# A chunked gated-linear-attention and adapter-mixture kernel: order of all engines from a list scheduler in the kernel, and the recurrent state kept in PSUM

## The chip, the cores and the metric

The kernel runs on one core of one Trainium2 chip. The metric is device time in microseconds (us) of one execution. The engines of the core are TensorE (PE: matmuls; PEld is its weight load), VectorE (DVE), ScalarE (ACT), GpSimd (POOL) and SyncE (SP, which here only issues DMA transfers). Each engine works through its own instructions strictly in the order in which the kernel emitted them, and waits where an input or a buffer is not ready. A *unit* below is one batch and one chunk of 128 time steps.

## The reference

Inputs are q, k, v and alpha, each of 4 batches x 8 heads x 768 steps x 48 elements, and the weights of a small mixture of adapters. Cut to what matters:

```python
for t in range(S):                                   # S = 768, per batch and head
    state = alpha[:, :, t, :, None] * state + k_t (x) v_t      # 48 x 48
    y[:, :, t] = q_t @ state
x = y as (3072, 384)                                 # 8 heads x 48
logits = x @ w_gate                                  # 8 experts, the best 2 kept
w = softmax of the two best logits
out = x + sum over chosen experts e of w_e * (x @ A[e]) @ B[e]   # rank 16
```

## The kernel before

There are 24 units: 4 batches of 6 chunks. Within a unit, `ln` takes log(alpha) on ACT, and `cum` sums the logs of later steps with one matmul against a triangular matrix `suf` (columns 0 to 383 of a PSUM tile) and the sum over the whole chunk with four matmuls against a column of ones. ACT makes `up` = exp(cum), `dn` = exp(-cum) and `dec` = exp(total). POOL makes `kg` = k*up (`kgm`), `qg` = q*dn (`qgm`) and a bf16 copy of v (`vbc`). PE transposes kg and qg, two heads at a time (`tr`, 8 transposes), DVE copies them out (`kq`), PE forms the 128 x 128 products of keys and queries of each head (`at`, 8 matmuls), DVE multiplies them by the causal mask into `at_sb` (`msk`).

The output of a unit, `y`, is a PSUM tile that collects three things: the query against the decayed state (`qs`, L292), the masked products against v (`av`, L303) and at the end the adapters' part (`delta`, L382). Between the second and the third lies a serial chain through three engines: `xb` (ACT) - `xt` (PE) - `xs` (ACT) - `z` (PE) - `zc` (ACT) - `mx`, `df` (DVE) - `ex` (ACT) - `wu`, `rd`, `zw` (DVE) - `zt` (PE) - `zs` (ACT) - `delta` (PE) - `fin` (ACT, the copy `o<-y`, L389) and the store (SP, L391). There are two buffers for y, one for `at`, five for o, and four shared ones in PSUM (tag "m") for cum, tr, kv, xt, z and zt.

The state: `kv` (L249) multiplies kg by v for two heads at once, so each of its four 128 x 96 results holds two wanted 48 x 48 blocks and two that mix heads. `state` (L262, L264) reads the wanted blocks with two DVE instructions (64 partitions x 192), adds `sdec` and writes them into the bf16 tile `sbd`, whose cross-head blocks were zeroed once. `sdm` (L221) makes `sdec` = sbd*dec on POOL. All of this occurs only where a chunk follows in the batch.

What sets the order: one list, `STEP`, of 32 pairs of a stage and an offset. Step n emits each stage for unit n + offset, so for instance step n holds `av` of unit n, `z` to `fin` of unit n-1, `tr` to `msk` of unit n+1 and the POOL products of units n+2 and n+3. Loads: batch 0 comes by chunk (24 transfers of 196.6 KB), batches 1 to 3 by tensor (alpha, k, q, v; 1.18 MB each). Eight chunk loads are issued from ACT after its table load, five weight loads and then all other loads of batch 0 and batch 1 from SP; from step 0 on each step appends one store and one more load to SP.

## Time and profile before

| | |
|---|---|
| three runs | 143.31, 142.85, 141.25 us; median 142.85 |
| the profiled execution | 143.36 us, of which the span from first to last instruction is 141.6 |
| busy in the span | PE 86.2 us, DVE 96.5, ACT 77.0, POOL 77.8 |
| DMA | 24.18 MB; read 19.28, written 4.72 |
| y copied out (`o<-y`), start | unit 0 at 33.11, unit 3 at 48.44, unit 20 at 126.58, unit 23 at 138.33 us |

The busy times are unions over the whole span, so they average a head that loads bound, a long middle and a tail. The start times of `o<-y` mark how far the units have come: 17 units pass between 48.44 and 126.58 us, 4.60 us each. In the views below, a line of the chain of waits has start, length and what the end of the program waited for; a group's line has instructions, busy time and mean nanoseconds of one, and the idle time in front with what ended it.

### The profile page before, as it was taken

How to read it: one execution, taken by the hardware profiler on the slowest of the kernel's cores; microseconds unless marked ns; L12 is line 12 of the kernel's file. 1: busy time of each engine (PE TensorE's matmuls, PEld its weight loads, DVE VectorE, ACT ScalarE, POOL GpSimd, SP SyncE). 2: the span in 40 equal slices, each digit the busy share in tenths (PEclk: the TensorE clock that was granted, in tenths of full speed). 3: DMA queues.
4: the chain of work that ended last, by engine and by line, in shares of the span. 5: the costliest groups of instructions: out<-in, count | busy, mean ns of one | idle time of the engine just before them, and what ended most of it. 6: DMA issues, size and time to landing. Idle time of an engine off the chain costs nothing.

```text
span 141.6 us, 2947 instructions
## 1 busy us (share of the span) xinstructions
PE 86.2 (61%) x1048; PEld 63.9 (45%) x1048; DVE 96.5 (68%) x236; ACT 77.0 (54%) x232; POOL 77.8 (55%) x111
## 2 busy tenths in 40 slices
PE   0002049919664997998868846577597649596330
PEld 0001037708443855866746624455374437473210
DVE  1110016946995687889889798789897998989530
ACT  3002545346582674776765857567467647555431
POOL 8000299618564775676785757748767478521200
PEclk9999999999995555555797799968959995959955
DMA  4999999968998829695985969892110111001111
GB/s 74 231 255 259 235 210 201 285 181 231 282 249 229 248 78 272 173 267 152 299 224 173 276 190 309 239 366 68 62 58 9 46 60 56 36 20 60 56 56 56
DMA packets 50718, 24.18 MB, mean 171 GB/s; under 512 B 29072, under 2 KB 50704, under 8 KB 50704
## 3 DMA queue, kind: packets, MB, share of 16 engines
q1 hardware_dynamic: 42384, 22.43, 58.1%
q10 hardware_dynamic: 8320, 1.57, 5.5%
q8 instruction: 8, 0.13, 0.4%
q14 instruction: 6, 0.05, 0.1%
HBM read 19.28 MB, written 4.72 MB: 169 GB/s over the span
## 4 chain that ended last, share of the span: by engine, by line
DVE 30%; DMA 19%; ACT 18%; SPq 16%; PE 9%; issue 5%; POOL 1%; ACTq 0%; POOLq 0%
SPq L88 8%; DVE kq L240 8%; SPq L91 8%; DVE zw L366 8%; DMA v_t<-in_v_dram 7%; DVE df L343 6%; ACT o L389 5%; DMA out_dram<-o 5%; ACT up L184 4%; DMA q_t<-in_q_dram 4%; PE zt L373 4%; DVE wu L354 3%; DMA W_st<-in_moe_A_dram 3%; ACT zc L333 3%; ACT zs L378 3%
## 5 line engine op out<-in xcount | busy, mean ns | idle before, releaser
L208 POOL TENSOR_TENSOR qg<-q_t,dn 128x384 bf16<-128x384 f32 x24 | 24.0, 999 | 23.8 <-ACT dn L189 23.8
L281 DVE TENSOR_TENSOR at_sb<-at,mask 128x1024 bf16<-128x1024 f32 x24 | 29.2, 1216 | 3.6 <-PE at L273 3.6
L240 DVE COPY kq<-tr 128x1024 bf16<-128x1024 bf16 x24 | 16.6, 690 | 13.1 <-PE tr L234 12.5
L221 POOL TENSOR_TENSOR sdec<-sbd,dec 128x384 bf16<-128x384 bf16 x20 | 16.6, 828 | 15.1 <-DVE sbd L264 12.9
L201 POOL TENSOR_TENSOR kg<-k_t,up 128x384 bf16<-128x384 f32 x24 | 24.0, 1001 | 0.9 <-ACT up L184 0.9
L215 POOL CAST vb<-v_t 128x384 bf16<-128x384 f32 x24 | 12.1, 503 | 14.0 <-PE kv L249 9.7
L173 PE MATMUL cum<-lg,suf 128*128 128x384 bf16 x24 | 10.9, 456 | 12.6 <-ACT lg L163 12.6
L234 PE MATMUL tr<-ident,kg 128*128 128x128 bf16 x96 | 12.9, 277 | 5.8 <-POOL kg L201 5.8
L378 ACT COPY zs<-zt 128x128 bf16<-128x128 bf16 x24 | 6.4, 266 | 16.5 <-PE zt L373 16.5
L273 PE MATMUL at<-kq 48*128 48x128 bf16 x192 | 12.1, 261 | 4.9 <-DVE kq L240 4.6
L348 ACT ACTIVATE ex<-df 128x8 f32<-128x8 f32 x24 | 5.0, 208 | 18.4 <-DVE df L343 18.4
L373 PE MATMUL zt<-ident,zw 128*128 128x128 bf16 x24 | 6.1, 254 | 14.4 <-DVE zw L366 14.4
L366 DVE SCALAR_TENSOR_TENSOR zw<-zc,rd,wu 128x128 bf16<-128x128 f32 x24 | 13.9, 580 | 0.8
L175 PEld LDWEIGHTS <-lg 128*128 128x128 bf16 x96 | 7.5, 116 | 14.0 <-issue 13.5
L292 PE MATMUL y<-sdec,kq 128*128 128x96 bf16 x80 | 8.3, 240 | 8.7 <-POOL sdec L221 8.0
L189 ACT ACTIVATE dn<-cum 128x384 f32<-128x384 f32 x24 | 11.5, 478 | 3.7 <-PE cum L175 3.5
L310 ACT CAST xb<-y 128x384 bf16<-128x384 f32 x24 | 11.4, 473 | 3.9 <-PE y L303 3.6
L264 DVE TENSOR_TENSOR sbd<-kv,sdec 64x192 bf16<-64x192 f32 x32 | 11.2, 351 | 3.1 <-PE kv L249 2.9
L234 PE MATMUL tr<-ident,qg 128*128 128x128 bf16 x96 | 12.7, 274 | 0.0
L389 ACT COPY o<-y 128x384 f32<-128x384 f32 x24 | 11.8, 494 | 1.6 <-PE y L382 1.0
L343 DVE TENSOR_SCALAR df<-zc,mx 128x8 f32<-128x8 f32 x24 | 11.7, 486 | 0.8
L184 ACT ACTIVATE up<-cum 128x384 f32<-128x384 f32 x24 | 12.2, 506 | 0.0
(45 smaller groups left out, 180.9 us busy)
## 6 DMA issues: line engine op xcount, KB each, us to landing
out_dram<-o SPq DMA_DIRECT2D x24, 192.0 KB, 2.5
v_t<-in_v_dram SPq DMA_DIRECT2D x5, 192.0 KB, 4.0
k_t<-in_k_dram SPq DMA_DIRECT2D x4, 192.0 KB, 3.7
q_t<-in_q_dram SPq DMA_DIRECT2D x4, 192.0 KB, 4.6
a_t<-in_alpha_dram ACTq DMA_DIRECT2D x3, 192.0 KB, 3.7
a_t<-in_alpha_dram SPq DMA_DIRECT2D x3, 192.0 KB, 3.8
k_t<-in_k_dram ACTq DMA_DIRECT2D x2, 192.0 KB, 4.9
q_t<-in_q_dram ACTq DMA_DIRECT2D x2, 192.0 KB, 4.3
```

Source lines behind the costliest of these rows:

```text
L184: nc.scalar.activation(s["up"].rearrange("p h d -> p (h d)"), s["cum"][:, 0:DM], AF.Exp)
L201: nc.gpsimd.tensor_tensor(out=s["kg"][:, :, 0:D], in0=batches[b][1][:, c], in1=s["up"], op=ALU.mult)
L208: nc.gpsimd.tensor_tensor(out=s["qg"][:, :, 0:D], in0=batches[b][2][:, c], in1=s["dn"], op=ALU.mult)
L215: nc.gpsimd.tensor_copy(out=s["vb"], in_=batches[b][3][:, c])
L221: nc.gpsimd.tensor_tensor(out=sdec[c % 2].rearrange("p a b d -> p a (b d)"), in0=sbd[c % 2].rearrange("p a b d -> p a (b d)"), in1=_bc(s[" ...
L234: nc.tensor.transpose(t[:, w, p, :], pair(src, p), ident[:, :])
L240: nc.vector.tensor_copy(out=s["kq"], in_=s["tr"])
L273: nc.tensor.matmul(t[:, hh, p, :], s["kq"][rows, 0, p, :], s["kq"][rows, 1, p, :], start=True, stop=True)
L281: nc.vector.tensor_tensor(out=s["at_sb"].rearrange("p a b t -> p (a b) t"), in0=s["at"].rearrange("p a b t -> p (a b) t"), in1=_bc_mid(mas ...
L343: nc.vector.tensor_scalar(s["df"], s["zc"][:, E * R:NW], s["mx"][:, 0:1], None, ALU.subtract)
L366: nc.vector.scalar_tensor_tensor(out=s["zw"], in0=s["zc"][:, 0:E * R].rearrange("p (e r) -> p e r", e=E), scalar=s["rd"][:, 0:1], in1=_bc( ...
L389: nc.scalar.copy(o, s["y"])
```

## The change

1. **Order.** `STEP` goes. A function `graph` lists each stage of each unit as a node with an engine, an occupancy and a latency in ns (`STAGES`), with data dependences (`CHAINS`) and buffer reuse (`RINGS`, `HOLDS`). `list_order` then simulates the engines: it repeatedly picks, on the engine that can start first, among the nodes that can start within 40 ns of the first one, the one with the lowest unit number less `LEAD` of its stage. The four shared PSUM buffers are handed out in that order. `plan` sorts everything by planned start, the loads by 7 us less than theirs, and the kernel emits in that order; stores become nodes of their own.
2. **State.** `state`, `sbd` and POOL's `sdm` go. `kv` now begins (for chunks 1 to 4) with one matmul of the identity against `sdec`, 128 x 384, and adds the four products onto it, so the PSUM tile holds the whole new state, cross-head blocks included. The next unit's `sdm` is one DVE product of that PSUM tile (128 x 384, f32) with a `dec` of 8 columns, into bf16 `sdec`. In the 8 columns, a small matmul of `sel` and `gap` puts -1000 where rows and head do not match, so exp gives 0 there.
3. **cum** also gets one matmul of 512 columns of zeros (`warm`) at its start, overwritten by what follows.
4. kg and qg have 4 buffers in place of 3; the first loads of k and v go on ACT, before the table load, all others on SP; the casts of the adapters' weights move behind `msk` of unit 1 on DVE.

In the order that results, y is worked on by pairs: in most of the list, ACT, for instance, has xb, xs, zc, ex, zs and o of one unit each beside the same stage of the next. On DVE a `kq`, `msk` or `sdm` stands between the pair's small instructions. Behind the six units of batch 0, DVE has kq, kq, msk, kq, msk of units 6 to 8 before the first instruction that needs v of batch 1. On SP, the store of unit 0 stands ahead of the loads of k and q of chunk 5, that of unit 1 ahead of v of chunk 5 and alpha, k and q of batch 1, those of units 2 and 3 ahead of v of batch 1; the stores of units 6 and 7 stand behind alpha of batch 3, and from unit 10 on only stores are left.

The diff, cut:

```diff
-RING = 3
+RING = 4
...
+STAGES = {
+    "ln": ("ACT", 445, 545), "ln2": ("ACT", 765, 865),
+    "cum": ("PE", 513, 680), "edn": ("ACT", 385, 485), "eup": ("ACT", 360, 485),
+    "edec": ("ACT", 98, 172), "kgm": ("POOL", 979, 1024), "qgm": ("POOL", 979, 1024),
+    "vbc": ("POOL", 419, 464), "tr": ("PE", 450, 620), "kq": ("DVE", 595, 679),
+    "sdm": ("DVE", 497, 581), "kv": ("PE", 340, 500), "at": ("PE", 400, 570),
+    "msk": ("DVE", 1164, 1248), "qs": ("PE", 170, 340), "av": ("PE", 215, 385),
+    "xb": ("ACT", 385, 485), "xt": ("PE", 170, 340), "xs": ("ACT", 360, 485),
+    "z": ("PE", 180, 350), "zc": ("ACT", 153, 278), "gmx": ("DVE", 91, 175),
+    "gdf": ("DVE", 76, 160), "gex": ("ACT", 107, 232), "gwu": ("DVE", 268, 352),
+    "grd": ("DVE", 71, 155), "gzw": ("DVE", 258, 342), "zt": ("PE", 57, 220),
+    "zs": ("ACT", 147, 272), "delta": ("PE", 163, 330), "fin": ("ACT", 385, 485),
+    "st": ("DMA", 655, 2455),
+}
+LEAD = {
+    "vbc": 4.27, "ln": 3.98, "cum": 4.66, "edn": 3.24, "eup": 2.43, "edec": 2.5, "kgm": 2.57,
+    "qgm": 3.55, "tr": 2.34, "kq": 0.1, "sdm": 0.93, "kv": 1.48, "at": -2.91, "msk": -0.66,
+    "qs": 0.66, "av": 0.85, "xb": 0.02, "xt": 0, "xs": 1.6, "z": 0.29, "zc": 1.6, "gmx": -0.26,
+    "gdf": 0.17, "gex": -0.25, "gwu": -0.88, "grd": -1.01, "gzw": 0.71, "zt": 2.42, "zs": 0.57,
+    "delta": -0.7, "fin": -3.99, "st": 100,
+}
+CHAINS = (
+    "ln cum eup kgm tr kq at msk av xb xt xs z zc gmx gdf gex gwu grd gzw zt zs delta fin st",
+    "cum edn qgm tr", "cum edec sdm kv", "kgm kv", "vbc kv", "sdm qs av", "kq qs", "vbc av",
+)
+RINGS = (
+    ("kgm", "eup", 2), ("qgm", "edn", 2), ("sdm", "edec", 6), ("tr", "kgm", RING), ("kv", "kgm", RING),
+    ("tr", "qgm", RING), ("kv", "vbc", 3), ("av", "vbc", 3), ("at", "kq", 3), ("qs", "kq", 3),
+    ("msk", "at", 1), ("av", "msk", 2), ("fin", "qs", 2), ("fin", "av", 2), ("xt", "xb", 3),
+    ("z", "xs", 3), ("delta", "zs", 3), ("st", "fin", 5), ("qs", "sdm", 2), ("kv", "sdm", 1),
+    ("kgm", "cum", 2), ("qgm", "cum", 2), ("at", "tr", 3), ("qs", "tr", 3), ("z", "xt", 3),
+    ("gzw", "z", 3), ("delta", "zt", 3), ("edec", "kv", -1), ("qs", "kv", 1),
+)
+HOLDS = {
+    "cum": (("eup", 0), ("edn", 0), ("edec", 0)), "tr": (("kq", 0),), "kv": (("sdm", 1),),
+    "xt": (("xs", 0),), "z": (("zc", 0),), "zt": (("zs", 0),),
+}
+SLOTS = 4
+READER = ("ln", "kgm", "qgm", "vbc")
+HANDOVER = {"PE": 53, "DVE": 35, "ACT": 35, "POOL": 35, "DMA": 600, "DMB": 600}
...
+def list_order(nodes, deps, holds):
...
+    slot, place, rel = [0] * SLOTS, {}, {}
...
+        best = None
+        for e, names in cand.items():
+            can = []
+            for n in names:
+                if n[0] == "ld" and loads[e][nl[e]][1] != n:
+                    continue
+                s = max(ready[n], free[e])
+                if n in holds:
+                    if slot[ns % SLOTS] is None:
+                        continue
+                    s = max(s, slot[ns % SLOTS])
+                can.append((s, n))
+            if can:
+                first = min(can)[0]
+                if best is None or first < best[0]:
+                    s, n = min((x for x in can if x[0] <= first + 40),
+                               key=lambda x: (nodes[x[1]][3], x[0]))
+                    if best is None or s < best[0]:
+                        best = (s, n, e)
+        if best is None:
+            return 1e9, order
+        s, n, e = best
+        cand[e].remove(n)
+        nl[e] += n[0] == "ld"
+        if n in holds:
+            place[n], slot[ns % SLOTS] = ns % SLOTS, None
+            ns += 1
...
+        for a in owner.get(n, ()):
+            left[a] -= 1
+            k = place[a]
+            rel[a] = max(rel.get(a, 0), end + 53)
+            if left[a] == 0:
+                slot[k] = rel[a]
+        for b in succ[n]:
+            eb = nodes[b][0]
+            if eb == e:
+                w = free[e] if e in ("PE", "DMA", "DMB") else end
+            else:
+                w = end + HANDOVER[eb]
+            ready[b] = max(ready[b], w)
+            wait[b] -= 1
+            if wait[b] == 0:
+                cand[eb].append(b)
...
+    return out[:8] + ["w"] + out[8:]
+
+
+def load_engine(x):
+    return "ACT" if x in ((0, 1, 0), (0, 3, 0)) else "SP"
...
+        for line in CHAINS:
+            names = line.split()
+            for f, g in zip(names, names[1:]):
+                dep((f, u if has(f, u) or f != "ln" else u - 1), (g, u))
+        for f, g, d in RINGS:
+            dep((f, u - d), (g, u))
+        dep(("kv", u - 1), ("sdm", u))
...
+        t = 1060 if c is not None else 4500
+        nodes[n] = ("DMB" if eng == "POOL" else "DMA", t, t + 1300, x)
...
+def plan(lead=LEAD):
+    nodes, deps, holds = graph(lead)
+    span, order = list_order(nodes, deps, holds)
+    start = {n: s for s, n in order}
+    before = {}
+    for a, b in deps:
+        before.setdefault(b, []).append(start[a])
+    keyed = []
+    for k, (s, n) in enumerate(order):
+        if n[0] == "ld":
+            if ("is", n[1]) in nodes:
+                continue
+            s = max([s - 7000] + before.get(n, []))
+        elif n[0] == "is":
+            n = ("ld", n[1])
+        keyed.append((s, k, n))
+    return span, [n for _, _, n in sorted(keyed)]
...
+    order = plan()[1]
+    early = [n for n in order if n[0] == "ld"][:8]
+    for n in early:
+        ld(n[1])
+    nc.scalar.preload_act_table_set("natural_log_exp_and_others")
...
+    def wcast(_):
+        nc.vector.tensor_copy(out=W, in_=W_st)
+        nc.vector.tensor_copy(out=B_all, in_=B_st)
...
+    sel = consts.tile([P, 2, HP], F2, name="sel")
+    nc.vector.memset(sel, 0.0)
+    gap = consts.tile([P, NP, 2], F2, name="gap")
+    nc.vector.memset(gap, 0.0)
+    for i in range(2):
+        nc.vector.memset(sel[HP * i:HP * i + 1, i, :], 1.0)
+        nc.vector.memset(gap[HP * i:HP * i + 1, :, 1 - i], -1000.0)
...
+    sdec = [consts.tile([P, NP, 2, D], F2, name=f"sdec{i}") for i in range(2)]
...
+        for _ in range(1):
+            nc.tensor.matmul(cum, suf[:, :], warm[:, :], start=True, stop=True)
         nc.tensor.matmul(cum[:, 0:DM], suf[:, :], lg[:, :, 0:D], start=True, stop=True)
+        nc.tensor.matmul(
+            cum[:, DM:DM + H], sel.rearrange("p a b -> p (a b)"),
+            gap.rearrange("p a b -> p (a b)"), start=True, stop=False,
+            skip_group_check=True)
         for p in range(NP):
             nc.tensor.matmul(
-                cum[:, DM + p:DM + p + 1],
+                cum[:, DM + 2 * p:DM + 2 * p + 2],
                 lg[:, 2 * p:2 * p + 2, :].rearrange("a b s -> a (b s)"), ones[:, :],
-                start=True, stop=True)
+                start=False, stop=(p == NP - 1), skip_group_check=True)
...
+        s["dec"] = scal.tile([P, H], F4, name="dec", bufs=6)
+        nc.scalar.activation(s["dec"], s["cum"][:, DM:DM + H], AF.Exp)
...
     def sdm(u):
-        s = st[u]
         b, c = units[u]
         if c > 0:
-            nc.gpsimd.tensor_tensor(
-                out=sdec[c % 2].rearrange("p a b d -> p a (b d)"),
-                in0=sbd[c % 2].rearrange("p a b d -> p a (b d)"),
-                in1=_bc(s["dec"][:, :], 2 * D), op=ALU.mult)
+            nc.vector.tensor_tensor(
+                out=sdec[c % 2].rearrange("p a b d -> p (a b) d"),
+                in0=st[u - 1].pop("kv").rearrange("p a b d -> p (a b) d"),
+                in1=_bc(st[u]["dec"][:, :], D), op=ALU.mult)
...
+        if c > 0:
+            nc.tensor.matmul(
+                s["kv"].rearrange("p a b d -> p (a b d)"), ident[:, :],
+                sdec[c % 2].rearrange("p a b d -> p (a b d)"),
+                start=True, stop=False, skip_group_check=True)
         for p in range(NP):
             nc.tensor.matmul(
                 s["kv"][:, p].rearrange("p b d -> p (b d)"), pair(s["kg"], p), pair(s["vb"], p),
-                start=True, stop=True)
-
-    def state(u):
-        s = st[u]
-        b, c = units[u]
-        if c + 1 == NCH:
-            return
-        for hh in range(2):
-            rows = slice(HP * hh, HP * hh + HP)
-            dst, src = sbd[(c + 1) % 2][rows, :, hh, :], s["kv"][rows, :, hh, :]
-            if c == 0:
-                nc.vector.tensor_copy(out=dst, in_=src)
-            else:
-                nc.vector.tensor_tensor(
-                    out=dst, in0=src, in1=sdec[c % 2][rows, :, hh, :], op=ALU.add)
...
+        if c == 0:
+            s["y"] = ps_y.tile([P, DM], F4, name="y")
...
-        o = outp.tile([P, DM], F4, name="o")
-        nc.scalar.copy(o, s["y"])
+        s["o"] = outp.tile([P, DM], F4, name="o")
+        nc.scalar.copy(s["o"], s["y"])
+
+    def store(u):
-        nc.sync.dma_start(out=out[t0:t0 + C, :], in_=o)
+        nc.sync.dma_start(out=out[t0:t0 + C, :], in_=st[u]["o"])
...
-    STEP = (
...
-    with tc.manual_schedule():
-        for n in range(-6, NU + 3):
-            for f, off in STEP:
-                u = n + off
-                if 0 <= u < NU:
-                    f(u)
-            for _ in range(1 if n >= 0 else 0):
-                if queue:
-                    load(*queue.pop(0))
+    for n in order:
+        if n not in early:
+            emit[n[0]](n[1])
```

## The prediction

> **What bounds the kernel now.** I read the slices of the span first, then the chain of waits in order of time, then the windows of a middle stretch, then the groups, and last single instructions in the timeline.
>
> The slices (3.54 us each) show two regimes:
>
> ```profile
> DVE  1110016946995687889889798789897998989530
> ...
> PEclk9999999999995555555797799968959995959955
> DMA  4999999968998829695985969892110111001111
> ```
>
> Up to about 44 us the DMA row is full while no engine is; from slice 14 on DVE is at 8 or 9 and the DMA row falls off. The chain names the hinge between the two, and one later stall:
>
> ```profile
> 34.23 10.04 DMA v_t<-in_v_dram
> 44.39 0.37 POOL vb L215
> 44.85 0.87 POOL sdec L221
> ...
> 82.85 7.03 DMA out_dram<-o
> 89.96 0.48 ACT o L389
> ```
>
> The first line: everything waits for v of batch 1, landed at 44.3 us. POOL, in order, holds `sdec` of unit 4 behind `vb` of unit 6, so the units of batch 0 wait for a load that they don't need: `o<-y` of unit 3 starts only at 48.44. The fourth line: a store queued behind loads holds an o buffer.
>
> Two stretches of the middle (us, busy time and count of PE, PEld, DVE, ACT, POOL, then clock, DMA share, GB/s):
>
> ```profile
> 50.00:82.00 32.00, 26.52 (x311) 19.98 (x310) 27.43 (x68) 22.23 (x69) 22.23 (x27) 0.65 0.74 216
> 91.60:126.00 34.40, 24.29 (x318) 18.04 (x319) 30.79 (x74) 21.31 (x69) 22.02 (x27) 0.82 0.25 85
> ```
>
> At 4.60 us a unit (front table), DVE's 86% and 90% are 3.94 and 4.12, mean 4.03 us a unit: it is the fullest engine, but it idles 0.57. The rest of the pace is in-order waiting; the chain there hops DVE - PE - ACT through the mixture. The groups that the change touches:
>
> ```profile
> L281 DVE TENSOR_TENSOR at_sb<-at,mask 128x1024 bf16<-128x1024 f32 x24 | 29.2, 1216 | 3.6 <-PE at L273 3.6
> ...
> L221 POOL TENSOR_TENSOR sdec<-sbd,dec 128x384 bf16<-128x384 bf16 x20 | 16.6, 828 | 15.1 <-DVE sbd L264 12.9
> ...
> L366 DVE SCALAR_TENSOR_TENSOR zw<-zc,rd,wu 128x128 bf16<-128x128 f32 x24 | 13.9, 580 | 0.8
> ...
> L264 DVE TENSOR_TENSOR sbd<-kv,sdec 64x192 bf16<-64x192 f32 x32 | 11.2, 351 | 3.1 <-PE kv L249 2.9
> ...
> L343 DVE TENSOR_SCALAR df<-zc,mx 128x8 f32<-128x8 f32 x24 | 11.7, 486 | 0.8
> ```
>
> L343 works on 8 columns and takes 486 ns in the mean; its shortest is 231 and its longest 754. L366 has 350 and 1105. The short ones lie beside an idle POOL, the long ones beside POOL products; L281 stays within 1210 to 1225 either way.
>
> **The change, part by part.** I sum up to the landing of v of batch 1, then 18 units at a pace, then the end.
>
> *Head, 47.6 us.* The bytes ahead of v of batch 1 decide. Before: 24 chunk loads (4.72 MB), batch 1 (4.72) and weights (0.4), 9.84 MB by 44.3 us; the window 13 to 44 us shows 240 GB/s, so this stretch is transfer alone. The change keeps these bytes and puts four stores (4 x 196.6 KB = 0.79 MB, 3.3 us at 240 GB/s) ahead of that v: 44.3 + 3.3 = 47.6. Bounds: 44.3 if stores cost the loads nothing; above, SP waits in order for the copies of y. It reached k of chunk 5 at 19.6 us; in the new order unit 0's copy I put at about 22 (first log at 4.5 instead of 12.0 us, since ACT no longer issues eight loads first; then the rows of its chain, 17 us with both casts and `msk` of unit 1 in front of `z`). Queued behind it are all later loads. 2.4 us there and as much at unit 1 give 52.4 if no backlog covers it; each transfer waits only for the one eight places ahead of it, so a backlog is likely, and I take 47.6.
>
> In exchange, the six units of batch 0 need no v of batch 1 any more. They begin some 8 us earlier, and 6 x 4.6 = 28 us from about 9 us plus one chain end near 40, inside the load wait. Before, only units 0 to 2 were out by then. The earlier start itself gains nothing beyond this: the load hides it.
>
> *State.* Removed: two DVE instructions in 20 units, 0.71 us together in the timeline (351 each), and POOL's 828 ns. Added on DVE: one product of 384 PSUM elements, not in the trace. Below: 0.351 (L264, 192 elements, also PSUM); above: 0.71, the two removed. Between L264 and L281 an element costs (1216 - 351)/(1024 - 192) = 1.04 ns, so 351 + 192 x 1.04 = 551 ns; I take that. Over 24 units: 20/24 x (0.551 - 0.71) = -0.13 us a unit (bounds -0.30 and 0). POOL loses 0.69 a unit, 16.6 in all; it was at 69% and isn't the bound, but its products stretch DVE: mean over shortest is 0.255 (L343), 0.07 (L354) and 0.23 (L366), 0.56 a unit. POOL's products fall from 2.69 to 2.0 us a unit, so by that share 0.14 goes (bounds 0 and 0.56). DVE: 4.03 - 0.13 - 0.14 = 3.76 us a unit.
>
> *PE.* By the shapes a unit streams 4764 columns; added are 512 (`warm`), 12 (`gap` and wider ones) and 16/24 x 384 (identity), 5544 in all. The timeline prices a column:
>
> ```profile
> 99.15 0.39 PE L234 MATMUL tr<-ident,kg 128*128 128x128 bf16 x4
> ...
> 104.04 0.63 PE L234 MATMUL tr<-ident,kg 128*128 128x128 bf16 x4
> ```
>
> One last matmul is 219 and 314 ns, so the starts lie 57 and 105 ns apart: 0.44 ns a column at full clock, 0.83 at half. 5544 columns are 2.4 or 4.6 us. At full clock this lies beside DVE; at half it is a bound of its own. Before, the clock stood at half from 41.9 to 69.2 us with PE busy for over 80% (the fives above), and then mostly full. With 16% more columns PE is nearly without a pause when cold, so I take full clock for most of the middle; the bounds are 0 and +0.87 us a unit (4.63 - 3.76).
>
> Here a rule is weighed: the Trainium skill, "TensorE: Matmul & The Clock Gate", Part 1, says that one window of about 3.4 us of sustained matmuls releases the throttle. This trace agrees only in part, since 27.3 us at over 80% did not release it. By the rule the sum below stands as it is; by the row taken to the end it becomes the cold rival.
>
> *Order.* Which limit is next? The y chain of a pair: two buffers, each held from `qs` to `fin`. By the groups and the timeline at full clock: 0.33 + 0.36 + 0.47 + 0.33 + 0.48 + 0.35 + 0.30 + 0.17 + 0.49 + 0.21 + 0.36 + 0.16 + 0.58 + 0.23 + 0.27 + 0.34 + 0.49 = 5.9 us. The last unit shows the handovers: from `zc` at 135.14 to the end of `o` at 138.81 is 3.67, its rows are 3.25, so 0.04 each; 16 make 0.6. The partner ahead on ACT costs about 0.47, and one DVE product in between (0.69 to 1.22) about 1.0. A pair takes 5.9 + 0.6 + 0.5 + 1.0 = 8.0, 4.0 a unit, above DVE's 3.76. Pace 4.0; bounds 3.76 (DVE without a gap) and 4.60 (the order gains nothing).
>
> The store stall at 82.85 goes: when SP meets the stores of units 6 and 7, four loads are queued ahead, and o has five buffers. It is inside the 4.60. `ident` and `warm` at cum cost DVE and ACT nothing at full clock; RING 4 and the moved casts are in the head.
>
> *Sum.* 47.6 + 0.6 (`vb`, 503 ns, and a handover) + 9 x 8.0 + 2.8 (end of the last `o` at 138.81 to the span's end) = 123.0; outside the span lie 143.36 - 141.6 = 1.76: 124.8 on the profiled execution's footing. The median is 0.4% below that execution, so **124.3 us**, forecast 124. Units 6 to 8 enter with some DVE work done; the last pairs have no DVE work beside them; I set neither off.
>
> **Rivals.**
> 1. *The order gains nothing* (18%): the planner's times are too short for the chip (`gzw` 258 against 580, `gdf` 76 against 486), so engines wait in order as now. 47.6 + 0.6 + 18 x 4.60 + 2.8 + 1.76 = 135.6. For: L343 and L366 vary by POOL; against: the waits of DVE are mostly for ACT within one unit's chain (10.5 us before `mx`), which pairing fills.
> 2. *DVE alone bounds, the stores are free* (14%): 44.3 + 0.6 + 18 x 3.76 + 2.8 + 1.76 = 117.1.
> 3. *PE stays at half clock* (8%): 4.63 us of columns a unit; between 53.08 and 67.14 us, all cold, three units passed at 4.69 against 4764 x 0.83 = 3.98 of columns, 1.18 times. 4.63 x 1.18 = 5.46, and 47.6 + 0.6 + 98.3 + 2.8 + 1.76 = 151: slower than before. It decides from a pace of (142.85 - 52.8)/18 = 5.0. For: that stretch; against: later windows are mostly full.
> 4. *The plan doesn't do what it says*: loads wait on stores at SP and the head grows to 52.4 or more. At pace 4.0 that is 129.6, inside my main case.
>
> **How the numbers follow.** Main case 118 to 131: 60%. The range reaches from rival 2 to rival 1 with its bounds: 115 to 136, leaving out rival 3, the slower half of rival 1 and a little below. A difference under 2% (140.0 to 145.7) can't be told from no change. Rival 3 gives slower 6% and part of same; same 4%; faster 90%.
>
> **What would show it.** Right: v of batch 1 landing at 45 to 50 us with units 0 to 5 copied out before; `o<-y` in pairs about 8 us apart; DVE near 94% in the middle; no L221 on POOL; the product of PSUM near 0.55 us; `df` shorter; full clock. Wrong: transposes 107 ns apart all through the middle (rival 3), `o<-y` 9 us apart a pair (rival 1), DMA idle before 45 us while SP waits for `o` (rival 4).

## The result and the profile after

| | before | after |
|---|---|---|
| median, us | 142.77 (4 runs, 141.25 to 143.31) | 167.25 (4 runs, 166.16 to 167.69) |
| span of the profiled execution, us | 141.6 | 164.4 |
| busy in the span: PE, DVE, ACT, POOL, us | 86.2, 96.5, 77.0, 77.8 | 98.2, 86.8, 79.5, 61.3 |
| v of batch 1, end of its last packet, us | 43.9 | 63.8 |
| last load, end of its last packet, us | 93.4 | 126.4 |

The ratio is 1.172, 95% interval 1.162 to 1.183: slower by 17%, where 124 us was forecast. The last two rows count the packets of the loads in order of time; the completion that an engine waits for comes at 44.3 and 65.4 us for v of batch 1, and at 93.8 and 127.2 for the last load. Executions more than 1.5% above the fastest of the same kernel are left out of all ratios here; the profiled ones of e3, g2, g4 and h1 below are such, so a difference of that size in their rows says nothing.

No engine got fuller: the busiest, PE, has 60% of the span. The slices of the kernel after (4.11 us each; the GB/s row is what the DMA engines moved):

```profile
DVE  1025756767120046656870389487547795768050
PEclk9999999879655558597895699598765985859555
DMA  6998999999999999969997999999999402020202
GB/s 104 163 146 145 175 141 181 213 201 164 170 157 169 206 184 168 165 167 184 167 165 151 162 164 188 191 169 182 180 187 234 153 0 100 0 96 0 96 0 96
```

The DMA row is at 9 in nearly all of the first 31 slices, some 127 us; before, the DMA engines were busy in the first 27, about 96 us, and not full in all of them. DVE never stays at 9. And the full DMA engines move only some 170 GB/s (169 in the median of those slices). The two stretches that were shown of before, in the same columns:

```profile
50.00:82.00 32.00, 19.35 (x233) 13.88 (x231) 15.41 (x30) 13.59 (x38) 13.93 (x17) 0.70 1.00 176
91.60:126.00 34.40, 23.66 (x304) 17.05 (x306) 23.17 (x53) 21.09 (x64) 16.93 (x21) 0.80 1.05 178
```

In the first, the DMA engines had a share of 0.74 at 216 GB/s before, now 1.00 at 176; DVE fell from 27.43 to 15.41 us of 32. The queue of the loads and stores (packets, MB, share of 16 engines' span), first before and then after:

```profile
q1 hardware_dynamic: 42384, 22.43, 58.1%
```

```profile
q1 hardware_dynamic: 48624, 23.61, 83.4%
```

The bytes are the same (q10 lost what q1 gained, since some first loads moved from ACT to SP), but 58.1% of 141.6 us is 82 us and 83.4% of 164.4 is 137. The chain of waits in order of time (start, length, what) has three long links:

```profile
41.01 16.03 DMA q_t<-in_q_dram
...
72.68 16.40 DMA q_t<-in_q_dram
...
109.64 9.88 DMA q_t<-in_q_dram
```

One for each of the batches 1 to 3. The groups say who waits, and that the operations themselves cost what they should:

```profile
L429 POOL TENSOR_TENSOR kg<-k_t,up 128x384 bf16<-128x384 f32 x24 | 24.0, 1000 | 37.1 <-DMA k_t<-in_k_dram 26.7 <-ACT up L410 10.3
L436 POOL TENSOR_TENSOR qg<-q_t,dn 128x384 bf16<-128x384 f32 x24 | 23.7, 998 | 16.6 <-DMA q_t<-in_q_dram 16.5
...
L448 DVE TENSOR_TENSOR sdec<-kv,dec 128x384 bf16<-128x384 f32 x20 | 11.0, 549 | 3.1 <-PE kv L481 3.1
...
L585 DVE SCALAR_TENSOR_TENSOR zw<-zc,rd,wu 128x128 bf16<-128x128 f32 x24 | 9.7, 404 | 0.6
...
L562 DVE TENSOR_SCALAR df<-zc,mx 128x8 f32<-128x8 f32 x24 | 9.0, 375 | 0.4
```

So the loads became slow at the same bytes. The trace records each packet, a piece of a transfer that one DMA engine moves at a time. The 768-byte ones (four runs of 192 bytes, loads of batches 1 to 3) took 42 ns in the median before and 79 after. The 192-byte ones (one run each, loads of batch 0) took 15 and 16 in the median, but 15.2 and 22.7 in the mean: before they are nearly all at 15, after they spread from 13 to 46. The 1536-byte ones of the stores took about 66 in the median of both. What changed is what writes into SBUF in 192-byte runs.

That points at the load tiles. They hold 192 of every 256 bytes (`load`, `[P, H * NCH, 64]` in f32). In the built programs they start in each partition at byte 35648 before and 37472 after, 64 and 96 beyond a multiple of 256. A run from 64 ends at 256; a run from 96 crosses it and ends at 288. The tiles ahead moved them by 1824 bytes: `warm` +1024, `sel` +256, two more `kg`/`qg` +2048, `sbd` gone -1536, and `gap`, 16 bytes that take 32. Only the last isn't a multiple of 256.

### The profile page after: what moved, and what is told of

The parts are those of the page before. It is cut to its first block, busy times and chain, and to the rows that moved or that the text cites. A ratio compares the mean times of both kernels' runs of the same rounds, so it can differ in the third digit from the quotient of the medians.

```text
span 164.4 us, 3023 instructions
## 1 busy us (share of the span) xinstructions
PE 98.2 (60%) x1106; PEld 67.5 (41%) x1112; DVE 86.8 (53%) x221; ACT 79.5 (48%) x228; POOL 61.3 (37%) x93
## 3 DMA queue, kind: packets, MB, share of 16 engines
q1 hardware_dynamic: 48624, 23.61, 83.4%
## 4 chain that ended last, share of the span: by engine, by line
DMA 30%; PE 23%; DVE 11%; ACT 11%; POOL 9%; SPq 7%; issue 7%; ACTq 0%; DVEq 0%; POOLq 0%
DMA q_t<-in_q_dram 26%; SPq L302 6%; POOL qg L436 5%; DMA a_t<-in_alpha_dram 4%; PE tr L461 4%; POOL kg L429 4%; PE y L601 3%; DVE wu L573 2%; PE y L522 2%; PE xt L535 2%; DVE at_sb L499 2%; DVE zw L585 2%; ACT xb L529 2%; PE cum L395 2%; PE y L509 2%
## 5 line engine op out<-in xcount | busy, mean ns | idle before, releaser
L461 PE MATMUL tr<-ident,qg 128*128 128x128 bf16 x96 | 12.8, 276 | 15.2 <-POOL qg L436 15.2
L540 ACT COPY xs<-xt 128x384 bf16<-128x384 bf16 x24 | 11.6, 482 | 10.4 <-PE xt L535 10.3
L461 PEld LDWEIGHTS <-qg 128*128 128x128 bf16 x96 | 8.9, 127 | 16.3 <-POOL qg L436 16.3
L557 DVE MAX8 mx<-zc 128x8 f32<-128x8 f32 x24 | 4.0, 166 | 18.2 <-ACT zc L552 18.0
L601 PE MATMUL y<-B_all,zs 128*128 128x384 bf16 x24 | 11.0, 458 | 3.8 <-ACT zs L597 3.8
L461 PE MATMUL tr<-ident,kg 128*128 128x128 bf16 x96 | 12.3, 267 | 1.6 <-POOL kg L429 1.3
L522 PE MATMUL y<-vb,at_sb 128*128 128x48 bf16 x192 | 10.6, 201 | 3.8 <-DVE at_sb L499 2.5
L546 PE MATMUL z<-W,xs 128*128 128x136 bf16 x72 | 10.1, 262 | 4.4 <-ACT xs L540 3.3
L535 PE MATMUL xt<-ident,xb 128*128 128x128 bf16 x72 | 10.2, 265 | 4.2 <-ACT xb L529 4.0
L448 DVE TENSOR_TENSOR sdec<-kv,dec 128x384 bf16<-128x384 f32 x20 | 11.0, 549 | 3.1 <-PE kv L481 3.1
L573 DVE SCALAR_TENSOR_TENSOR wu<-zc,mx,ex 128x8 f32<-128x8 f32 x24 | 9.3, 388 | 5.4 <-ACT ex L567 5.3
```

Source lines behind the costliest of these rows:

```text
L461: nc.tensor.transpose(t[:, w, p, :], pair(src, p), ident[:, :])
L522: nc.tensor.matmul(s["y"][:, h * D:(h + 1) * D], s["at_sb"][:, hh, p, :], s["vb"][:, h, :], start=(c == 0 and h == 0), stop=False, skip_gr ...
L535: nc.tensor.transpose(s["xt"][:, i, :], s["xb"][:, i * P:(i + 1) * P], ident[:, :])
L573: nc.vector.scalar_tensor_tensor(out=s["wu"], in0=s["zc"][:, E * R:NW], scalar=s["mx"][:, 1:2], in1=s["ex"], op0=ALU.is_ge, op1=ALU.mult, ...
L601: nc.tensor.matmul(s["y"], s["zs"][:, :], B_all[:, :], start=False, stop=True, skip_group_check=True)
```

## Experiments 1 to 4: where the load tiles lie

A tile that nobody reads moves the load tiles, and with them every tile that is allocated behind it, by as many bytes. Apart from the one memset of that tile, no instruction and no order changes. With 112 elements it is 224 bytes:

```diff
+    shift = consts.tile([P, 112], F2, name="shift")
+    nc.vector.memset(shift, 0.0)
     suf = consts.tile([P, P], F2, name="suf")
```

The others differ in the size: 16 elements (32 bytes) and 96 (192) in the kernel after, 16 in the kernel before.

> The changed kernel, with an unused tile of 224 bytes per partition ahead of its other constants, so that the load tiles start at 64 modulo 256 bytes in their SBUF partition, where they stood before the change; in the changed kernel they start at 96. Nothing else differs, and no computation is left out. Theory 'place': the start of the 192-byte runs that the loads write sets the DMA rate. Then 768-byte packets take 42 ns again in the median (79 in the changed kernel), loads move at about 240 GB/s, v of batch 1 lands near 48 us and the time falls from 167 to between 118 and 136 us. Rival 'queue': it is the new issue order (nearly all loads on SP, stores in between) that slows the packets. Then they still take near 79 ns and the time stays within 163 to 170 us.

> The changed kernel with an unused tile of 32 bytes in the same place: the load tiles start at 128 modulo 256 bytes. No computation is left out. The runs then start at a multiple of 64 bytes, as before the change, but each of them (192 bytes long, 256 apart) has a multiple of 256 inside it. If a multiple of 64 is what counts, the time is that of the kernel with base 64 (118 to 136 us). If the 256-byte boundary counts, packets stay near 79 ns and the time near 167 us. By the rival 'queue', 167 us too.

> The changed kernel with an unused tile of 192 bytes in the same place: the load tiles start at 32 modulo 256 bytes. No computation is left out. The runs don't start at a multiple of 64 bytes, as in the changed kernel, but no multiple of 256 lies inside one (they end at 224). If a multiple of 64 is what counts, packets stay near 79 ns and the time near 167 us. If only the 256-byte boundary counts, 118 to 136 us. If both halves of a run that is off a multiple of 64 cost something, in between.

> The kernel before, with an unused tile of 32 bytes per partition ahead of its other constants: the load tiles start at 96 modulo 256 bytes instead of 64, as in the changed kernel. No computation is left out. Theory 'place': the packets of 768 bytes go from 42 to about 79 ns, v of batch 1 lands near 58 us instead of 44.3, and the loads last to about 120 us; the middle is then bound by loads too, and the time is 160 to 175 us. Rival 'queue': nothing changes, 141 to 144 us.

Measured (start of the load tiles modulo 256; median of the 768-byte packets; ends of last packets, and median times, in us):

```
kernel           start  run crosses 256  packet ns  v of batch 1  last load  time    ratio to before
before              64  no                  42          43.9         93.4    142.43
e1 (after)          64  no                  42          51.1         95.6    139.19  0.984 (0.972 to 0.995)
e3 (after)          32  no                  42          51.1         95.7    140.89  0.987 (0.981 to 0.992)
after               96  yes                 79          63.8        126.4    167.25  1.172 (1.162 to 1.183)
e2 (after)         128  yes                 79          64.3        126.3    166.36  (2 runs: 164.73, 167.99)
e4 (before)         96  yes                 79          63.0        125.0    175.26  1.239 (1.226 to 1.251)
```

The queue of e4 in the profile (before's hand-written order with the loads at 96):

```profile
q1 hardware_dynamic: 42384, 22.43, 78.0%
```

Multiples of 64 don't decide (128 is slow, 32 is fast); whether a 192-byte run crosses a multiple of 256 does. (A boundary at 512, which every second run would cross at 96 and 128, would order these four starts in the same way; no run here tells the two apart.) The tiles of the stores moved along, and their packets stay at 65 to 67 ns in the median of all six kernels. The effect needs nothing else of the change: the kernel before, moved by 32 bytes, loses 33 us. At equal place the change is a gain both times: 139.2 against 142.4 at 64, 167.3 against 175.3 at 96.

The Trainium skill has a rule that bears on it, in "DMA: Bandwidth & Descriptors", section "How a descriptor splits into AXI transactions": transactions are of up to 256 bytes, and a read must start one at a 256-byte-aligned address, so that a piece which starts elsewhere begins at the boundary below. By it a run of 192 bytes at 32 or 64 is one transaction, at 96 or 128 two. The rows agree with that count, 42 against 79 ns a packet. The page states it for reads, and its price is the count of 32-byte beats, with the unused bytes in front: by that an estimate is 7, 8, 9 and 10 beats for starts at 32, 64, 96 and 128. The measured 42, 42, 79 and 79 ns don't follow the beats. These are writes into SBUF, and no run here shows the transactions themselves.

So 27.5 us of the span (164.4 - 136.9) are the place. But e1 and e3 miss the 118 to 136 us that their expectations gave. That leaves the question why e1, with the place restored, has 136.9 us of span and not the 123.0 of the prediction.

## Experiments 5 to 8: the parts of the change, with the loads at 64

f1 is the kernel before with the state part alone (`sdm` on DVE from PSUM, the identity matmul, `sel` and `gap`; `STEP` loses only `(state, 0)`), with the tile of e1, since its own `gap` shifts what follows as it does in the kernel after. f2 is e1 without the matmul of `warm`. f3 gives the planner shorter load times, nearer to the trace (820 ns is one chunk's 196.6 KB at 240 GB/s). f4 is f3 with occupancies nearer to the trace (`cum` 620, `tr` 550, `kv` 420 and `at` 470 in place of 513, 450, 340 and 400, and the lines shown) and `LEAD` searched anew for them. The core of each edit, in this order:

```diff
-            nc.gpsimd.tensor_tensor(
-                out=sdec[c % 2].rearrange("p a b d -> p a (b d)"),
-                in0=sbd[c % 2].rearrange("p a b d -> p a (b d)"),
-                in1=_bc(s["dec"][:, :], 2 * D), op=ALU.mult)
+            nc.vector.tensor_tensor(
+                out=sdec[c % 2].rearrange("p a b d -> p (a b) d"),
+                in0=st[u - 1].pop("kv").rearrange("p a b d -> p (a b) d"),
+                in1=_bc(st[u]["dec"][:, :], D), op=ALU.mult)
```

```diff
-            nc.tensor.matmul(cum, suf[:, :], warm[:, :], start=True, stop=True)
```

```diff
-            nodes[n] = ("DMA", 4000, 5300, x)
+            nodes[n] = ("DMA", 2400, 3700, x)
...
-        t = 1060 if c is not None else 4500
+        t = 820 if c is not None else 4500
```

```diff
-    "gdf": ("DVE", 76, 160), "gex": ("ACT", 107, 232), "gwu": ("DVE", 268, 352),
-    "grd": ("DVE", 71, 155), "gzw": ("DVE", 258, 342), "zt": ("PE", 57, 220),
+    "gdf": ("DVE", 240, 320), "gex": ("ACT", 107, 232), "gwu": ("DVE", 300, 400),
+    "grd": ("DVE", 71, 155), "gzw": ("DVE", 380, 470), "zt": ("PE", 57, 220),
```

> The kernel before with the state part of the change alone (kv keeps the state in PSUM through the identity matmul, sdm is one DVE product of it, dec has 8 columns), in the hand-written order, without warm, and with an unused tile of 224 bytes so that the loads start at 64 modulo 256 bytes as before. No computation is left out. By the sums of the prediction DVE loses 0.13 us a unit of its own work and up to 0.14 of stretching, 0.27 x 20 = 5 us at the most if all of it were on the path: 137 to 142 us. Rival: the product now waits on DVE for dec and kv in front of the mixture's small instructions, and the hand-written order makes that wait part of each step: 144 to 150 us.

> The changed kernel with its loads at 64 modulo 256 bytes (139.2 us), less the matmul of 512 zero columns in cum, whose result nothing reads. Theory 'clock': that matmul keeps TensorE's clock up; without it the mean granted clock falls from 0.86 to 0.80 or less and the time rises to 141 to 145 us. Rival 'load': it is only work, 0.43 us at half clock and 0.22 at full in PE's in-order queue 24 times, mostly beside other waits; without it the clock stays near 0.86 and the time falls to 136 to 139 us.

> The changed kernel with its loads at 64 modulo 256 bytes (139.2 us), with two numbers of the planner's table changed: a chunk load takes 820 ns instead of 1060, and the weights 2400 instead of 4000, which is nearer to what the trace shows (196.6 KB at 240 GB/s). The planner then puts the transposes of unit 2 ahead of the end of unit 0's mixture chain on PE, and one store between the loads of batch 1 at a time. Theory 'slow loads in the plan': batch 0's last copy of y, at 49.25 us with the old order, comes at 42 to 45, the first pair of batch 1 ends 4 to 7 us earlier than at 66.2, and the time is 132 to 136 us. Rival: v of batch 1 (landed at 51.1) and POOL behind it set the first pair anyway: 137.5 to 140 us.

> As the run with changed load times, and the planner's table also with longer times for what POOL stretches on DVE (df 240 instead of 76, wu 300 instead of 268, zw 380 instead of 258) and for PE at a mixed clock (cum 620, tr 550, at 470, kv 420 instead of 513, 450, 400, 340), and the priorities LEAD searched anew against that table. Theory 'wrong costs': with truer costs the pace in batches 1 to 3, 4.13 us a unit, comes to 3.8 to 4.0, and the time to 128 to 133 us. Rival: the pace is set by DVE, ACT and the two buffers of y whatever the order: 4.1 us a unit again, and the time equals that of the run with changed load times alone.

Measured, against 141.68 us of before beside them: f1 139.95 (ratio 0.989, 0.981 to 0.996), f2 139.64 (0.979, 0.968 to 0.990; between its two expectations), f3 138.05 (0.977, 0.968 to 0.985), f4 138.28 (0.974, 0.965 to 0.983). The four intervals overlap.

The state part alone is worth about 1%, and DVE's busy time falls from 96.5 to 83.8 us, without `STEP` gone. `warm` does nothing that can be measured in the time; e1's median is 139.19. The granted clock of the profiled executions by slices, e1 and then f2:

```profile
PEclk9999999995995559999999995999959959599555
```

```profile
PEclk9999999999999999996899955959959959599555
```

Means 0.863 and 0.877. But over the four executions of each the clock is 0.803 to 0.863 with the 512 columns a unit (median 0.82) and 0.771 to 0.877 without (median 0.78), so whether they raise it stays open. f3 brings the last `o<-y` of batch 0 from 49.25 to 42.1 and the first of batch 1 from 63.29 to 58.03, but the end moves by 0.6 (span 136.9 to 136.3). Truer costs (f4) don't make the pace faster: units 7 to 23 pass in 4.33 us each ((133.17 - 63.93)/16), against 4.24 in e1. So rival 1's reason, planned times too short for the chip, isn't shown to hold it: longer ones, with the priorities searched anew, gain nothing over f3. The expected 132 to 136 us of f3 and 128 to 133 of f4 are missed.

## Experiments 9 to 12: loads in the way, or the buffers of y

g1 and g2 leave out loads (batches 2 and 3, and also 1); their units read an earlier batch's tiles again, so that part of the output is not computed (the edit of g1 is shown; g2 has `b >= 1` and `batches[0]`). g3 gives y a third buffer in PSUM at the cost of one of the four shared ones (tag "m" has 3 in each of its stages); g4 is g3 with f3's load times.

```diff
         name, src = SRC[i]
+        if b >= 2:
+            batches[b][i] = batches[1][i]
+            return
```

```diff
-    ("msk", "at", 1), ("av", "msk", 2), ("fin", "qs", 2), ("fin", "av", 2), ("xt", "xb", 3),
+    ("msk", "at", 1), ("av", "msk", 2), ("fin", "qs", 3), ("fin", "av", 3), ("xt", "xb", 3),
...
-SLOTS = 4
+SLOTS = 3
...
-    ps_y = ctx.enter_context(tc.tile_pool(name="ps_y", bufs=2, space=PS))
+    ps_y = ctx.enter_context(tc.tile_pool(name="ps_y", bufs=3, space=PS))
```

> The changed kernel with its loads at 64 modulo 256 bytes (139.2 us), leaving out the loads of batches 2 and 3: their units compute on the tiles of batch 1, so the output of these batches is not the reference's. The order on every engine is the same. Theory 'y chain': the pace of batches 1 to 3 is the chain that each of the two y buffers is held for; a pair of units still takes 8.2 to 8.7 us and the time stays at 137 to 140 us. Rival 'loads in the middle': POOL and ACT, in order, hold earlier units behind products that wait for a later batch; without these loads the middle speeds up and the time falls to 130 to 134 us.

> The same, leaving out the loads of batch 1 too (batches 1 to 3 compute on the tiles of batch 0). If the head is bound by the landing of batch 1, as predicted, the first pair of batch 1, at 63.3 and 65.7 us with its loads, is copied out before 52 and the time falls by 10 us or more. If batch 0's own pace in the planned order sets the head (its last copy of y was at 49.25), the last copy of batch 0 stays at 45 to 49, the first pair comes at 56 to 60, and the time falls by 5 to 8 us.

> The changed kernel with its loads at 64 modulo 256 bytes (139.2 us), with three PSUM buffers for y and three shared ones (two and four before), and the planner told so; nothing is left out. Theory 'y chain': with three units in flight the pace of the middle falls from 4.1 to 4.2 us a unit to 3.7 to 3.9, where DVE is next, and the time to 130 to 135 us. Rival: the shared PSUM buffers become the bound, and the time is 138 to 145 us.

> As the run with three y buffers, with the planner's load times also changed as in the run with changed load times (820 ns a chunk, weights 2400 ns). If the head gain there (5 us) was given back because two y buffers bound the middle, it is kept now: 125 to 131 us. If it was given back to the loads of batches 2 and 3, the time is that of three y buffers alone, within 2 us.

Measured, against 142.07 us of before beside them: g1 139.11 (ratio 0.981, 0.973 to 0.990), g2 140.83 (2 runs), **g3 131.06 (0.924, 0.918 to 0.930)**, g4 131.02 (0.921, 0.914 to 0.929).

e1's time isn't in its loads. In g2, with no load behind batch 0 at all, the last `o<-y` of batch 0 starts at 50.11 and the first two of batch 1 at 64.31 and 66.38; in e1 at 49.25, 63.29 and 65.67. What sets the head is the order. Neither expectation of g2 allowed for that: both had the first pair at 60 us or sooner, and the time at least 5 us shorter. e1's PE at unit 0 (start, length; columns as in the timeline):

```profile
19.71 0.50 PE L603 MATMUL y<-B_all,zs 128*128 128x384 bf16 x1
20.00 0.63 PE L463 MATMUL tr<-ident,kg 128*128 128x128 bf16 x4
20.43 0.63 PE L463 MATMUL tr<-ident,qg 128*128 128x128 bf16 x4
```

The transposes of unit 2 stand in the list behind unit 0's `delta`, the end of its whole chain. The planner held the chunk loads for slower (1060 ns each) than they are (0.82 us at 240 GB/s) and put the chain first; f3, with 820, has the copy `kq` of unit 2 at 17.95 in place of 21.10, and the head is 5 to 7 us shorter. POOL further on in e1:

```profile
36.91 0.56 POOL L445 CAST vb<-v_t 128x384 bf16<-128x384 f32 x1
44.53 0.99 POOL L431 TENSOR_TENSOR kg<-k_t,up 128x384 bf16<-128x384 f32 x1 [7.06 <-ACT up L412]
...
53.63 0.99 POOL L431 TENSOR_TENSOR kg<-k_t,up 128x384 bf16<-128x384 f32 x1
54.57 1.40 POOL L445 CAST vb<-v_t 128x384 bf16<-128x384 f32 x3
```

POOL waits 7.06 us for `up` of unit 6, which ACT has in its list behind work of batch 0 (in g2, with no load to wait for, that `up` starts no earlier, at 44.81), and the copy of v of batch 1, landed at 51.1, starts at 54.57 behind products in POOL's own order.

In the middle, the two buffers of y hold the pace, as far as g3 shows. The windows of e1 and then of g3 (length, then busy us and count of PE, PEld, DVE, ACT, POOL, clock, DMA share, GB/s):

```profile
60.00:82.00 22.00, 14.66 (x232) 10.38 (x231) 18.87 (x51) 15.75 (x48) 14.24 (x17) 1.00 0.88 252
82.00:100.00 18.00, 13.21 (x186) 9.53 (x183) 13.76 (x35) 13.70 (x41) 9.79 (x13) 0.89 0.70 211
100.00:126.00 26.00, 18.03 (x226) 12.95 (x227) 18.70 (x53) 13.26 (x40) 6.28 (x9) 0.81 0.11 39
```

```profile
60.00:82.00 22.00, 16.11 (x248) 11.97 (x248) 20.22 (x50) 16.73 (x55) 14.11 (x17) 1.00 0.85 252
82.00:100.00 18.00, 14.17 (x179) 10.10 (x179) 14.82 (x39) 12.19 (x36) 6.53 (x8) 0.81 0.65 197
100.00:126.00 26.00, 17.39 (x240) 11.49 (x237) 19.37 (x58) 15.82 (x51) 8.55 (x12) 0.90 0.15 56
```

With two buffers no engine is full: DVE has 86%, 76% and 72%. With three the first stretch rises to 92%, and units 7 to 23 pass in 3.77 us each ((125.82 - 65.54)/16) against 4.24 in e1 ((133.59 - 65.67)/16). g3 beats both kernels: it is the planned order, the state in PSUM, the loads at 64 and a third y. The planner makes a new order for three buffers, so that what g3 gains belongs to the buffer and its order together; no run here separates them.

g4 shows again what f3 showed, an earlier head that is lost further on: its first copies of batch 1 come at 58.79 and 62.10 (g3: 62.72 and 65.54), but unit 8 at 70.24 (69.93).

## Experiments 13 and 14: where the shorter head goes

f3 and g4 without the loads of batches 2 and 3, by the edit of g1.

> f3_plan_loads with the loads of batches 2 and 3 left out: their units read batch 1's tiles again, so their part of the output is not computed. The four stores of batch 0 and all loads of batches 0 and 1 stay. Theory 'loads': the 5 us that the head gained (last o of batch 0 at 42.1 in place of 49.25, first pair at 58.03 in place of 63.29) are given back because the order now runs ahead of batch 2's loads, k of batch 2 at 58.8 above all, for which POOL waits 4.93 us at 59.4 with the v copy of unit 9 behind it: then the first pairs stay near 58 and 60, the pair behind them comes near 64 and 65 in place of 68.28 and 69.09, and the time falls from 138 to about 133 to 135. Theory 'order': the list gives the gain back by itself, its later pairs stand at a worse spacing: then 68 and 69 stay within 1 us and the time stays between 136.5 and 139.

> g4_three_y_plan_loads with the loads of batches 2 and 3 left out in the same way. In g4 the first pair of batch 1 came at 58.79 and 62.10 against 62.72 and 65.54 in g3, but unit 8 at 70.24 against 69.93. Theory 'loads': the three buffers for y take the order further ahead of the loads, so without these loads unit 8 comes near 65 and the time falls from 131 to 126 to 128. Theory 'order': unit 8 stays near 70 and the time between 129.5 and 132.

Measured, against 141.22 us of before beside them: h1 136.62 (ratio 0.964, 0.957 to 0.971), h2 124.80 (0.884, 0.878 to 0.889).

With three buffers it was the loads. POOL in g4, then in h2:

```profile
60.68 1.98 POOL L431 TENSOR_TENSOR kg<-k_t,up 128x384 bf16<-128x384 f32 x2 [4.93 <-PE zt L594]
68.04 2.90 POOL L438 TENSOR_TENSOR qg<-q_t,dn 128x384 bf16<-128x384 f32 x3 [5.38 <-DMA q_t<-in_q_dram]
```

```profile
61.11 1.01 POOL L434 TENSOR_TENSOR kg<-k_t,up 128x384 bf16<-128x384 f32 x1 [2.11 <-ACT up L415]
62.08 1.97 POOL L441 TENSOR_TENSOR qg<-q_t,dn 128x384 bf16<-128x384 f32 x2
66.20 1.00 POOL L441 TENSOR_TENSOR qg<-q_t,dn 128x384 bf16<-128x384 f32 x1 [2.15 <-ACT dec L428]
```

In g4, k of batch 2 lands at 60.0 and q at 67.5, by the ends of their last packets, and the products start 0.6 us behind each. (The first line names `zt` as releaser; with k in at 60.0, the DMA is the likelier one.) Without these loads unit 8 comes at 66.59 in place of 70.24, and 6.2 us of the time go. That is somewhat more than the 3 to 5 us that the expectation of the loads gave, and far from no change. From v of batch 2 (72.4) to v of batch 3 (95.4), g4's loads take 23.0 us for six units, 3.83 each, with the DMA engines at a share of 0.84 between 72 and 95 us: with three y the engines (3.77 in g3) are about as fast as the loads come.

With two buffers it is mostly the order. h1 gains 1.4 us where the expectation of the loads was 3 to 5, and the pair of units 8 and 9 comes at 69.70 and 70.58, no earlier than in f3 (68.28 and 69.09). How the two buffers give the gain back, instruction by instruction, stays open.

## Why the prediction was wrong, point by point

Between the predicted span, 123.0, and the measured one, 164.4, lie 41.4 us: 27.5 of place (after against e1), 10.0 in the head of e1 (the first pair of batch 1 ends at 66.2, predicted 47.6 + 0.6 + 8.0 = 56.2), and 3.9 of pace (eight more pairs to 134.07, 8.49 each for 8.0). The end, 2.8, was right.

- **The step that failed: "The change keeps these bytes", priced at 240 GB/s.** The bytes are kept; the rate isn't. In the stretch that the prediction read, before and then after (columns as in the windows above):

```profile
13.00:44.00 31.00, 18.64 (x218) 14.24 (x217) 17.78 (x40) 16.59 (x50) 17.94 (x22) 0.97 0.98 240
13.00:44.00 31.00, 20.98 (x234) 14.20 (x236) 19.28 (x47) 15.69 (x46) 10.62 (x14) 0.91 1.13 178
```

  178 GB/s in place of 240, and v of batch 1 complete at 65.4 us, not 47.6. The prediction took the rate for a property of the transfers, and no rival had it change. The diff alone shows its cause, the new tiles of `warm`, `sel` and `gap` and a lost `sbd`, but I priced them as work, not as a move of what is allocated behind them. With the rate of before the answer would have been faster, as forecast, but by 1.6% (e1; 0.5 to 2.8%) and not by 13.
- **Head, loads.** With the place restored, v of batch 1 lands at 51.1: inside 44.3 to 52.4, near the upper bound, but not for its reason. The copies of units 2 and 3 ended at 38.9, before SP came to their stores at 39.77; SP's three issues between 28.45 and 44.3 us took 5.78, 4.99 and 4.50 us, and the first two are loads, which need no copy. f3, with another order of stores and loads on SP, has 47.1. But g2 shows that this landing wasn't what the units waited for.
- **Head, "one chain end near 40, inside the load wait".** Wrong by 9: the last copy of batch 0 starts at 49.25 in e1. The sum took 4.6 us a unit from about 9 us on, a pace of the middle, without reading the list for what stands behind `delta` of unit 0. This is the 10 us.
- **State.** Right: the product of 384 PSUM elements measured 0.549 us, predicted 0.551. DVE's total fell from 96.5 to 87.2 us in e1, 0.39 a unit, predicted 0.27. `df` went from a mean of 486 ns to 391 and `zw` from 580 to 476, 0.20 a unit together: the relief from POOL was sized too small (0.14 for three groups). It can't be read from POOL's share alone: with the state part alone (f1) `df` falls to 234 ns and `zw` rises to 630, and DVE's total falls by 0.53 a unit, so it matters which instruction the order puts beside a POOL product. (Nor did all short ones lie beside an idle POOL: of the 13 `zw` of 350 to 353 ns before, 8 had a POOL product beside a third of their time.)
- **Order, the y chain.** Right as the next limit, short in size: 8.49 us a pair for 8.0. From the start of `xb` to the end of `o`, the rows with handovers, partner and one DVE product gave 7.29; e1 has 7.53 in the mean of units 8 to 23. g3, with a third buffer and the order planned for it, lifts the limit. DVE "near 94% in the middle" fails with it: 86%, 76% and 72% in the three windows.
- **DVE alone, 3.76 a unit.** As a bound it was too high: h2 has 3.58 a unit ((119.71 - 62.36)/16), with DVE at 94% (20.62 of 22 us) between 60 and 82 us. That g3 has 3.77 agrees by chance, since its DVE share is 92%, 82% and 75%.
- **Store stall.** Gone, as said: nothing like the 7.03 us at 82.85 is in e1's chain.
- **PE, full clock.** Not all through. In e1 slices 13 to 15 and 25 are at half, and from the thirtieth on slow ones stand between full ones. The cold rival wasn't the cause of the pace: in e1's window 60 to 82 the clock is 1.00 and PE is busy for 14.66 of 22 us. In the kernel after, both prices of a column stand side by side, as before:

```profile
66.66 0.60 PE L461 MATMUL tr<-ident,kg 128*128 128x128 bf16 x4
...
71.47 0.39 PE L461 MATMUL tr<-ident,kg 128*128 128x128 bf16 x4
```

  (A start every 105 ns is 0.82 ns a column, and 5544 columns are then 4.56 us, not 4.63; the bound of +0.87 would be +0.80, and rival 3's 5.46 stays, since the price cancels in it.)

- **Rivals.** 4 named the right resource, transfers, but the wrong mechanism (loads queued behind stores) and a price of 5 us. The rival that ended slower, the cold PE, had 8%; the slower result came from a cause that had none. That h2's span is 123.0 too confirms nothing: it has a later head and a faster pace than the sum, and leaves half the loads out.

## What to carry to other kernels

When a change adds, removes or resizes a tile, look where the tiles written by DMA now start: with runs of 192 bytes, a start at 96 in place of 64 beyond a multiple of 256 was worth 28 and 33 us of some 140, more than anything that the change did on the engines. Compare the median time of packets of the same size in the two traces before reading any wait: it tells a slower transfer from a later one in one number. And when no engine is full and no load is late, count the buffers of the longest chain: one more y, with the order planned for it, was worth 8 us, where truer planning costs or fewer loads alone were worth about 1 or none.

## What the runs showed of the hardware

- A 192-byte run written into SBUF across a multiple of 256 bytes costs about twice one that stays inside, in the median of packets of four: 79 against 42 ns. The stream moved 178 GB/s in place of 240 between 13 and 44 us, the DMA engines full in both. In the packets of a single run the mean grew from 15.2 to 22.7 ns and many stayed at 15. Being a multiple of 64 is neither needed (32) nor enough (128).
- Small DVE instructions can stretch beside POOL's products by factors: `df` on 8 columns takes 0.22 to 0.23 us in all 15 units of e1 where it has no such product beside it, and 0.22 to 1.15 in the other 9. The products that read PSUM stay at 0.55 (`sdec`) and 1.22 (`msk`) either way.
- A matmul of 512 columns of zeros in each unit brought no time (139.19 us with it, 139.64 without), and the granted clock of four executions each overlaps: 0.803 to 0.863 with it, 0.771 to 0.877 without.
